# Sixteen units in rounded parts, a chain moved to VectorE at the start, and one function moved to GpSimd at the end

## The chip, the cores and the metric

The kernel runs on one core of a Trainium2 chip. The metric is the device time of one execution in microseconds (us). The core's engines are TensorE (PE in the profile, with PEld for its weight loads), VectorE (DVE), ScalarE (ACT), GpSimd (POOL) and SyncE (SP, which starts most DMAs). Each engine works through its own list of instructions in order; an instruction that waits holds up everything behind it on that engine.

## What is computed

Three pieces follow one another: a linear attention with a delta rule, a network with a rational activation, and a network with a squared relu. Cut to what matters:

```python
# q, k, v: (4, 8, 768, 48); beta: (4, 8, 768)
k_n = k / (norm(k, axis=-1) + 1e-6)
for t in range(768):                       # state: (4, 8, 48, 48)
    y[t]  = q[t] @ state
    state = state + beta[t] * outer(k_n[t], v[t] - k_n[t] @ state)
x = y.transpose(0, 2, 1, 3).reshape(3072, 384)
# network 1: w_in (384, 2048), w_out (2048, 384)
h = x @ w_in
P = a0 + a1*h + a2*h**2 + a3*h**3
Q = 1 + |b0|*|h| + |b1|*h**2
x = (P / (Q + 1e-6)) @ w_out
# network 2: its own w_in, w_out of the same shapes
out = relu(x @ w_in)**2 @ w_out
```

## The kernel before

**Tiles and units.** The 3072 tokens are 6 tiles of 512; the 2048 hidden columns are 16 units of 128. For each tile and unit, the h product (`mm1`, L932) makes a 128x512 block of h in a PSUM bank, an elementwise chain turns it into g, and a second product (`mm2_1`) adds g times the unit's slice of w_out to three banks that hold the tile's output. I write "unit 5.0" for unit 0 of tile 5; tiles are numbered 0 to 5, so tile 5 is the last. Network 2 does the same with a shorter chain, after network 1's last tile.

**Rounded parts.** TensorE multiplies full fp32 operands slowly. So an operand is split into a rounded part and the remainder, each of which is in a faster format, and a product is three products of parts: the h product is 9 matmuls of 128x512 (six with `xh`, three with `xl`). The second product of network 1 is done in one of two ways. In the f32 form (L983) it is three full fp32 matmuls, which the trace counts as six. In the parts form (L986) it is nine, and needs `ph` (ACT, L966) and `pl` = g - ph (POOL, L967), and the parts of w_out, `E` and `F`. The table `QS` says, for each four units, from which tile on the parts form is used: units 0 to 3 from tile 1, units 4 to 11 from tile 2, and units 12 to 15 never.

**The chain of network 1** (`rational`), for each tile and unit: |h| on ACT (L949); its linear function b = b1|h| + b0 on ACT (L950); c = a linear function of h on ACT or DVE (L952, L357); b times |h| on POOL (L955); two DVE instructions on c (L956, L957); Ln and Exp on ACT for 1/Q (L958, L959); three DVE instructions that end with g (L960, L961, L962). L962 is also the last to read the h bank, so the bank is free for another h product then.

**Attention** is cut into groups of 8 steps. Each group's keys are normalised (L477 to L487, on DVE, the longest L486), a small triangular inverse is built step by step (L494 and L498, on POOL for all groups but the first), goes out through memory and comes back transposed as `TN` (L337 on SP), and then TensorE forms W (L570) and T21 (L584), on which the attention steps rest. These steps are spread over tiles 0 to 4.

**Weights.** Network 1's `raw` and network 2's `raw` and `rb` buffers are loaded by DMA as words and split into parts: a copy and a shift (L867, L868), merges on DVE (L872, L876), rounded copies on ACT (L881, L889), subtractions on POOL (L883, L890).

**What sets the order.** A planner (class `Plan`) takes each task with its engine, an assumed cost, a due time and the buffers that it needs, plays the program several times and fixes each engine's order in advance; the program is then written out in that order. Shared buffers, PSUM banks among them, are given out by the planner too. A change in a cost, an engine or a due time so moves many instructions.

Of the kernel before, what the change touches and what calls it, by code (L numbers as in the profile page):

```python
# [36 lines left out]
QS = (1, 2, 2)  # L37
# [8 lines left out]
def tm(u):  # L46

    return T0 + U1 * u if u < 96 else T2 + U2 * (u - 96)
# [192 lines left out]
def kernel(ctx, tc, kT, kS, qT, kn, vn, beta, par_in, w1, w2, outT):  # L241
# [40 lines left out]

    def words(kind, q):
        return lambda: held(kind, q, f"Q{q}", [128, 2 * DM], w1.dtype)[:, :]
# [14 lines left out]
    home = {0: 2, 5: 0, 6: 1, 7: 3}  # L299
    PL.pool("raw2", [lambda y=y: late["raw"][y] for y in range(2)] + [words("rb", q) for q in range(4)])  # L300
    for j, q in home.items():
        slot["raw", 2, j] = PL.pools["raw2"][2 + q]
        PL.gives["raw", 2, j] = [("raw2", 2 + q)]

# [537 lines left out]
    def weights(l, j, due, duo, slack):  # L842
# [7 lines left out]
        wait = [] if l == 1 else [PL.last["late"]] if j not in home else free2[(7, 11, 0, 15)[home[j]]] if j else parts  # L850
# [36 lines left out]
        if l == 2:  # L887
            used[rk] = [len(PL.tasks) - 1, len(PL.tasks) + 1]
            add("ACT", 0.52, lambda: A_.copy(late["C"][j][:, si], res(so)), r=[rk, "late"], w=[("C", j)], due=duo)  # L889
            add("POOL", 1.15, lambda: P_.tensor_tensor(late["C"][j][:, so], res(so), late["C"][j][:, si], op=ALU.subtract),  # L890
                r=[rk], w=[("C", j)], due=duo, lock=1, free=[rk])

# [49 lines left out]
    def rational(i, j, due):  # L942
# [7 lines left out]
        add("ACT", 0.83, lambda: A_.activation(b(), a(), AF.Identity, bias=s(4), scale=s(5)), r=[ak, "par"], w=[bk], due=due + 3.3, alloc=(("b",), bk))  # L950
# [21 lines left out]
    def mm2_1(i, j, due):  # L972
        gk, pk, mk = ((x, (i, j, 1)) for x in ("g", "ph", "pl"))
        two = i >= SJ.get(j, NT)
        if two and i == SJ[j]:
            add("ACT", 0.52, lambda: A_.copy(Ew(j), Bw(j)), r=[("B", j), "pairs"], w=[("E", j)] + [("B", x) for x in range(4 * (j // 4) - 4, 4 * (j // 4)) if x >= 0], due=due - 3)
            add("POOL", 1.15, lambda: P_.tensor_tensor(late["F"][j], Bw(j), Ew(j), op=ALU.subtract), r=[("B", j), ("E", j)], w=[("F", j)], due=due - 2, lock=1)
            parts.append(len(PL.tasks) - 1)
        for d in range(NK):
            def go(d=d):  # L980
                e = slice(128 * d, 128 * d + 128)
                if not two:
                    M.matmul(acc[d], Bw(j)[:, e], slot[gk], start=(j == 0), stop=(j == NJ - 1))  # L983
                    return
                for m, (a, b) in enumerate(((Ew(j)[:, e], slot[mk][0]), (late["F"][j][:, e], slot[pk][0]), (Ew(j)[:, e], slot[pk][0]))):
                    M.matmul(acc[d], a, b, start=(j == 0 and m == 0), stop=(j == NJ - 1 and m == 2))  # L986
# [33 lines left out]
    def pairs():  # L1020
# [4 lines left out]
        late["F"] = {j: sp.tile([128, DM], F32R, name=f"F{j}") for j in SJ}  # L1025
# [38 lines left out]
    for j in range(NJ):  # L1064
        weights(2, j, tm(96 + j) - 3, tm(96 + j) + 9, SA - SB * j)
# [91 lines left out]
```

## Time and profile before

| what | value |
|---|---|
| median of 3 runs | 1034.88 us (1034.8 to 1035.22) |
| the profiled execution | 1035.71 us |
| its span, first to last instruction | 1034.0 us |
| mean granted TensorE clock | 0.965 of full speed |
| PE busy | 976.6 us, 94% |
| DVE / ACT / POOL busy | 689.8 / 597.8 / 450.7 us |
| first h product of the last tile starts | 556.43 us |
| third h product of network 2 starts | 636.28 us |

The times of the rows are microseconds from the span's start. The profiled execution is 0.83 us above the median, and 1.7 us of it lie outside its span.

### The profile page before, as it was taken

What the parts mean: (1) busy time and instruction counts of PE and PEld (TensorE: products, weight loads), DVE (VectorE), ACT (ScalarE), POOL (GpSimd) and SP (SyncE); (2) the same over time, 40 slices, a digit from 0 to 9 for tenths busy, and PEclk for the clock granted to TensorE, in tenths of its full rate; (3) what the DMA queues carried; (4) which work ended last, traced back from release to release, by engine and by line L of the source; (5) the groups of instructions that cost most, each with busy time, mean ns of one, the idle gap of its engine ahead of it and who ended that gap; (6) DMA issues with size and microseconds to landing.
All of it is one profiled execution on the core that took longest, in us unless ns stands there. A gap on an engine that the chain in (4) does not pass through costs nothing.

```text
span 1034.0 us, 23206 instructions
## 1 busy us (share of the span) xinstructions
PE 976.6 (94%) x9532; PEld 754.2 (73%) x9532; DVE 689.8 (67%) x1129; ACT 597.8 (58%) x1047; POOL 450.7 (44%) x543
## 2 busy tenths in 40 slices
PE   4675999999999999999999998999999999999998
PEld 4574666577568867877886765888888888888886
DVE  6888978986788798788885899873343433433332
ACT  4465667876677687577766887743242333333322
POOL 1189987598489849954442656630000000000000
PEclk8567999999999999999999999999999999999999
DMA  8674568315803541250103016500010000000000
GB/s 246 175 212 125 111 207 223 61 53 152 158 33 83 156 71 50 72 124 32 34 5 126 1 54 238 198 30 32 1 61 1 28 35 1 20 11 1 31 1 31
DMA packets 126922, 84.84 MB, mean 82 GB/s; under 512 B 95648, under 2 KB 111776, under 8 KB 126816
## 3 DMA queue, kind: packets, MB, share of 16 engines
q1 hardware_dynamic: 126688, 83.26, 29.4%
q8 instruction: 75, 1.23, 0.5%
q14 instruction: 31, 0.25, 0.1%
q10 hardware_dynamic: 128, 0.10, 0.0%
HBM read 63.54 MB, written 18.61 MB: 79 GB/s over the span
## 4 chain that ended last, share of the span: by engine, by line
PE 75%; DVE 8%; POOL 6%; issue 5%; ACT 3%; DMA 2%; SPq 1%; ACTq 0%; POOLq 0%; DVEq 0%
PE bank L932 32%; PE bank L986 9%; PE bank L667 8%; PE bank L1015 6%; PE bank L1013 6%; PE bank L1014 6%; PE bank L983 6%; POOL mem L955 2%; DVE Tt L498 1%; DVE tmp L494 1%; POOL Tt L498 1%; POOL tmp L494 1%; PE bank L570 1%; POOL pl L967 1%; SPq L337 1%
## 5 line engine op out<-in xcount | busy, mean ns | idle before, releaser
L932 PE MATMUL bank<-xh,A 128*128 128x512 f32 x1152 | 311.8, 406 | 13.4 <-DVE mem L962 8.0
L932 PEld LDWEIGHTS bank<-xh,A 128*128 128x128 f32 x1152 | 217.0, 190 | 78.3 <-issue 10.6
L955 POOL TENSOR_TENSOR mem<-mem 128x512 f32<-128x512 f32 x96 | 126.1, 1314 | 116.5 <-ACT mem L950 114.8
L1001 DVE SCALAR_TENSOR_TENSOR mem<-bank,mem 128x512 f32<-128x512 f32 x96 | 66.2, 689 | 149.5 <-ACT mem L1000 149.1
L932 PE MATMUL bank<-xl,A 128*128 128x512 f32 x576 | 163.3, 392 | 0.0
L1000 ACT ACTIVATE mem<-bank 128x512 f32<-128x512 f32 x96 | 57.5, 598 | 154.0 <-PE bank L932 153.9
L983 PE MATMUL bank<-mem,B 128*128 128x512 f32 x264 | 127.0, 613 | 2.9 <-DVE mem L962 2.9
L932 PEld LDWEIGHTS bank<-xl,A 128*128 128x128 f32 x576 | 109.0, 189 | 23.3
L1015 PE MATMUL bank<-gh,C 128*128 128x512 f32 x288 | 113.8, 395 | 0.0
L1004 DVE TENSOR_TENSOR gl<-mem,gh 128x512 fp32r<-128x512 f32 x96 | 71.3, 744 | 63.4 <-ACT gh L1003 63.3
L1013 PE MATMUL bank<-gl,C 128*128 128x512 f32 x288 | 113.5, 394 | 0.0
L1014 PE MATMUL bank<-gh,C 128*128 128x512 f32 x288 | 111.9, 389 | 0.0
L1003 ACT CAST gh<-mem 128x512 fp32r<-128x512 f32 x96 | 59.6, 621 | 75.8 <-DVE mem L1001 62.0
L498 POOL TENSOR_TENSOR Tt<-Tt,tmp 128x31 f32<-128x31 f32 (+15 forms) x155 | 88.1, 568 | 9.8
L494 POOL TENSOR_TENSOR tmp<-Gb,Tt 128x31 f32<-128x31 f32 (+15 forms) x155 | 84.3, 544 | 16.8 <-DVE nT L485 7.9
L960 DVE SCALAR_TENSOR_TENSOR mem<-mem,par,bank 128x512 f32<-128x512 f32 x96 | 71.2, 742 | 27.0 <-ACT bank L959 26.3
L949 ACT ACTIVATE mem<-bank 128x512 f32<-128x512 f32 x96 | 56.9, 593 | 52.7 <-PE bank L932 39.4
L958 ACT ACTIVATE mem<-mem,par 128x512 f32<-128x512 f32 x96 | 69.3, 722 | 29.0 <-POOL mem L955 28.5
L983 PEld LDWEIGHTS bank<-mem,B 128*128 128x128 f32 x264 | 48.9, 193 | 48.5 <-issue 39.0
L956 DVE TENSOR_TENSOR mem<-bank,mem 128x512 f32<-128x512 f32 x96 | 65.8, 686 | 20.5 <-ACT mem L952 10.5
L950 ACT ACTIVATE mem<-mem,par 128x512 f32<-128x512 f32 x96 | 78.1, 813 | 2.1
L967 POOL TENSOR_TENSOR pl<-mem,ph 128x512 fp32r<-128x512 f32 x52 | 67.5, 1299 | 26.3 <-ACT ph L966 13.9
(129 smaller groups left out, 1725.9 us busy)
## 6 DMA issues: line engine op xcount, KB each, us to landing
raw<-in_w_dram SPq DMA_DIRECT2D x16, 768.0 KB, 6.1
rb<-in_w_dram SPq DMA_DIRECT2D x10, 768.0 KB, 4.5
X<-in_qT_dram SPq DMA_DIRECT2D x48, 112.0 KB, 2.9
gs<-Gs SPq DMA_DIRECT2D x40, 128.0 KB, 2.8
kn<-in_kn_dram SPq DMA_DIRECT2D x12, 384.0 KB, 4.5
vn<-in_vn_dram SPq DMA_DIRECT2D x12, 384.0 KB, 4.2
y<-mem SPq DMA_DIRECT2D x18, 256.0 KB, 2.0
out_dram<-mem SPq DMA_DIRECT2D x18, 256.0 KB, 2.0
```

What stands on the lines that cost most here:

```text
L494: E_.tensor_tensor(tv, _mid(Gb[:, s, s + 1:32], [128, a, b]), Tt[:, 0:a, s:s + 1].to_broadcast([128, a, b]), op=ALU.mult)
L498: E_.tensor_tensor(Tt[:, 0:a, s + 1:32], Tt[:, 0:a, s + 1:32], tv, op=ALU.subtract)
L667: M.matmul(*y[:3], start=a, stop=z)
L932: M.matmul(h, a, b, start=(m == 0), stop=(m == len(seq) - 1))
L950: add("ACT", 0.83, lambda: A_.activation(b(), a(), AF.Identity, bias=s(4), scale=s(5)), r=[ak, "par"], w=[bk], due=due + 3.3, alloc=(("b", ...
L955: add("POOL", 1.32, lambda: P_.tensor_tensor(b(), b(), a(), op=ALU.mult), r=[ak], w=[bk], due=due + 4.2, lock=1)
L967: add("POOL", 1.3, lambda: P_.tensor_tensor(slot[mk][0], g(), slot[pk][0], op=ALU.subtract), r=[gk, pk], w=[mk], due=due + 11.5, lock=1, a ...
L983: M.matmul(acc[d], Bw(j)[:, e], slot[gk], start=(j == 0), stop=(j == NJ - 1))
L986: M.matmul(acc[d], a, b, start=(j == 0 and m == 0), stop=(j == NJ - 1 and m == 2))
L1013: M.matmul(acc[d], wh, gl, start=(j == 0), stop=False)
L1014: M.matmul(acc[d], wl, gh, start=False, stop=False)
L1015: M.matmul(acc[d], wh, gh, start=False, stop=(j == NJ - 1))
```

## The change

Five things are edited.

1. `QS` gets a fourth entry, 3: units 12 to 15 use the parts form from tile 3 on, so in tiles 3, 4 and 5. Their `E` and `F` lie in storage that other weights have left (`Fw`), and are made in tile 3's reach with two buffers of the attention as scratch.
2. In tile 0, for units 0 to 2, the product b times |h| goes to DVE instead of POOL.
3. In the last tile the linear function of |h| goes to POOL (`tensor_scalar`) instead of ACT.
4. The normalisation of attention group 2 waits for the tasks in the list `opened`, which held only the splitting of tile 0's x; the g of units 0.0 and 0.1 is added to it (`OPEN`). And the attention's tasks are entered one tile further ahead.
5. Network 2's unit 0 of weights is loaded early into the first part of `xin`, the buffer of network 1's x, after the last tile's x has been split; the x of network 2's first tile, which goes there too, waits for its use.

```diff
-QS = (1, 2, 2)
+QS = (1, 2, 2, 3)
+OPEN = 2
+X0 = 83
...
+    def Fw(j):
+        return held("F", 3, "Q3", [128, 4 * DM], F32R)[:, DM * (j - 12):DM * (j - 12) + DM] if j > 11 else late["F"][j]
...
-    home = {0: 2, 5: 0, 6: 1, 7: 3}
+    home = {5: 0, 6: 1, 7: 3, 8: 2}
...
+    xw = xin.rearrange("p k n -> p (k n)")[:, 0:1536]
+    slot["raw", 2, 0] = xw.bitcast(w1.dtype) if f64 else xw[:, :2 * DM]
...
+        if i == NT - 1:
+            add("POOL", 1.3, lambda: P_.tensor_scalar(b(), a(), s(5), s(4), op0=ALU.mult, op1=ALU.add), r=[ak, "par"], w=[bk], due=due + 3.3, lock=1, alloc=(("b",), bk))
+        else:
+            add("ACT", 0.83, lambda: A_.activation(b(), a(), AF.Identity, bias=s(4), scale=s(5)), r=[ak, "par"], w=[bk], due=due + 3.3, alloc=(("b",), bk))
...
-        add("POOL", 1.32, lambda: P_.tensor_tensor(b(), b(), a(), op=ALU.mult), r=[ak], w=[bk], due=due + 4.2, lock=1)
+        dv = i == 0 and j < 3
+        add("DVE" if dv else "POOL", 0.69 if dv else 1.32, lambda: (V if dv else P_).tensor_tensor(b(), b(), a(), op=ALU.mult), r=[ak], w=[bk], due=due + 4.2, lock=1)
...
+        if i == 0 and j < OPEN:
+            opened.append(len(PL.tasks) - 1)
...
-        if two and i == SJ[j]:
+        if two and i == SJ[j] and j == 12:
...
+            for x in range(12, 16):
+                keys = [("Gb", 0, o) for o in (0, 32, 64, 96)] if x < 14 else [("Tt", 0)]
+                add("ACT", 0.52, lambda x=x: A_.copy(Ew(x), Bw(x)), r=[("B", x), "pairs"], w=[("E", x)] + [("B", y) for y in range(8, 12)], due=due - 9)
+                add("POOL", 1.15, lambda x=x: P_.tensor_tensor(T[x - 12], Bw(x), Ew(x), op=ALU.subtract), r=[("B", x), ("E", x)], w=keys, due=due - 8, lock=1)
...
+                add("ACT", 0.52, lambda x=x: A_.copy(Fw(x), T[x - 12]), r=keys, w=[("F", x)] + over, due=due - 5)
...
+    attention(0)
     for i in range(NT):
-        attention(i)
-        attn_last = len(PL.tasks)
         split(i, 1, tm(16 * i) - 3)
+        if i < NT - 1:
+            attention(i + 1)
+            attn_last = len(PL.tasks)
```

**How it moves instructions.** Lines after the change are numbered higher by 7 at the attention (L486 becomes L493, L570 L577, L584 L591), by 9 at the h product (L932 becomes L941), by 13 in the chain (L955 becomes L968, L962 L975), L966 and L967 become L981 and L982, and L983 and L986 become L1008 and L1011.

The first place is the opening of tile 0 on DVE. `bank_74` and `bank_72` hold the h of units 0.0 and 0.1, `Gb_120` the keys of attention group 2. Before, in part:

```order
L956 TENSOR_TENSOR mem<-bank_74,mem 128x512
L477 RECIPROCAL nbr<-tmp_124 128x32
...
L486 TENSOR_TENSOR Gb_120<-Gb_120,nbr 128x1024
L487 COPY Tt_122<-nbr 128x32
L485 STREAM_TRANSPOSE nT_131<-tmp_124 128x32
L957 SCALAR_TENSOR_TENSOR mem<-mem,par,bank_74 128x512
```

After the change:

```order
L969 TENSOR_TENSOR mem<-bank_74,mem 128x512
L968 TENSOR_TENSOR mem<-mem 128x512
L970 SCALAR_TENSOR_TENSOR mem<-mem,par,bank_74 128x512
L968 TENSOR_TENSOR mem<-mem 128x512
L969 TENSOR_TENSOR mem<-bank_72,mem 128x512
...
L975 SCALAR_TENSOR_TENSOR mem<-bank_74,mem 128x512
L975 SCALAR_TENSOR_TENSOR mem<-bank_72,mem 128x512
L484 RECIPROCAL nbr<-tmp_124 128x32
```

The normalisation now stands behind the g of both units, and DVE makes the products b times |h| (L968) itself.

The same place on PE. `A_85`, `A_86` and `A_87` are the weights of units 0.1, 0.2 and 0.3, and `TT`, `TN` belong to the attention's W. Before, the first matmul of each product and what follows:

```order
L932 MATMUL bank_72<-xh_100,A_85 128x512 x2
...
L932 MATMUL bank_73<-xh_100,A_86 128x512 x2
...
L932 MATMUL bank_74<-xh_100,A_87 128x512 x2
...
L932 MATMUL bank_73<-xl_105,A_89 128x512
L570 MATMUL bank_76<-TT_118,TN 32x32 x64
```

After the change:

```order
L941 MATMUL bank_72<-xh_100,A_85 128x512 x2
...
L941 MATMUL bank_74<-xh_100,A_86 128x512 x2
...
L941 MATMUL bank_72<-xh_100,A_87 128x512 x2
...
L1008 MATMUL bank_71<-mem,B_923 128x512
L577 MATMUL bank_75<-TT_118,TN 32x32 x64
L941 MATMUL bank_74<-xh_100,A_88 128x512 x2
```

Unit 0.2 now takes bank 74, which unit 0.0 must have left, where it had a third bank; and W comes two h products (units 0.4 and 0.5) earlier in the order, before unit 0.4 instead of after unit 0.5.

The second place is the turn from tile 4 to the last tile on PE. Before, the last h product of tile 4 ends in `bank_72`, and these follow it up to the last tile's first h product in `bank_76`; `E_3402`, `F` and `B_2202` are slices of w_out. In part:

```order
L932 MATMUL bank_72<-xl_105,A_99 128x512
L986 MATMUL bank_69<-pl_2397,E_3402 128x512
...
L986 MATMUL bank_70<-ph_2396,E_3402 128x512
L983 MATMUL bank_69<-mem,B_2202 128x512
...
L983 MATMUL bank_70<-mem,B_2202 128x512
L932 MATMUL bank_76<-xh_100,A_84 128x512 x2
```

There stand 15 matmuls of the parts form and 12 of the f32 form (4 units), so that tile 4 is complete before tile 5 starts. After the change:

```order
L941 MATMUL bank_72<-xl_105,A_99 128x512
L1011 MATMUL bank_69<-pl_2444,E_3544 128x512
...
L1011 MATMUL bank_71<-ph_2443,E_3544 128x512
L941 MATMUL bank_76<-xh_100,A_84 128x512 x2
```

Now 18 matmuls of the parts form (2 units) stand there and none in f32; two more units of tile 4 come after the last tile's first h products.

The third place is the end of the last tile on POOL. Before:

```order
L955 TENSOR_TENSOR mem<-mem 128x512
L967 TENSOR_TENSOR pl_2397<-mem,ph_2395 128x512
L955 TENSOR_TENSOR mem<-mem 128x512
L967 TENSOR_TENSOR pl_2398<-mem,ph_2396 128x512
L955 TENSOR_TENSOR mem<-mem 128x512 x3
L883 TENSOR_TENSOR A_84<-rb_3496,A_84 128x384
```

After:

```order
L960 TENSOR_SCALAR mem<-mem,par 128x512
L968 TENSOR_TENSOR mem<-mem 128x512
L982 TENSOR_TENSOR pl_2444<-mem,ph_2442 128x512
L982 TENSOR_TENSOR pl_2445<-mem,ph_2443 128x512
...
L890 TENSOR_TENSOR A_85<-raw_0_6801,A_85 128x384
L982 TENSOR_TENSOR pl_2444<-mem,ph_2442 128x512
L890 TENSOR_TENSOR A_86<-raw_1_6802,A_86 128x384
L897 TENSOR_TENSOR C_6780<-raw_0_6801,C_6780 128x384
L982 TENSOR_TENSOR pl_2445<-mem,ph_2443 128x512
```

From the first linear function (L960) to that last `pl`, POOL has 16 linear functions, 16 products (L968), 17 subtractions for `pl` (L982) and 5 subtractions for weights of network 2 (L890, L897).

## Rows read from the trace of the kernel before

**Rows 1.** The page, busy time of each engine, share of the span and instructions.

```profile
PE 976.6 (94%) x9532; PEld 754.2 (73%) x9532; DVE 689.8 (67%) x1129; ACT 597.8 (58%) x1047; POOL 450.7 (44%) x543
```

**Rows 2.** Windows of tiles 3, 4, 5: length, busy PE, PEld, DVE, ACT, POOL; clock.

```profile
375.90:464.90 89.00, 87.84 (x1187) 67.57 (x1185) 74.64 (x127) 62.19 (x106) 69.89 (x92) 1.00 0.29 72
464.90:556.40 91.50, 91.34 (x923) 68.11 (x918) 74.08 (x123) 64.02 (x110) 35.95 (x28) 1.00 0.10 30
556.40:628.70 72.30, 66.90 (x271) 50.58 (x269) 62.06 (x87) 63.59 (x102) 39.75 (x31) 0.98 0.18 61
```

**Rows 3.** The chain that ended last, in tile 4: start, us, what.

```profile
476.54 2.58 PE bank L983 x6
479.11 2.08 PE bank L932 x9
481.19 2.04 PE bank L986 x9
483.24 2.04 PE bank L932 x9
```

**Rows 4.** PE's waits from 85 to 640: us in total, times, longest.

```profile
PE bank L932 <- DVE mem L962: 8.0, 3, 7.4
PE bank L986 <- POOL pl L967: 3.9, 4, 2.0
```

**Rows 5.** Timeline of PE in the opening of tile 0.

```profile
99.69 2.93 PE L932 MATMUL bank<-xh,A 128*128 128x512 f32 x6 [7.44 <-DVE mem L962]
...
114.41 1.29 PE L570 MATMUL bank<-TT,TN 32*32 32x32 f32 x128
```

**Rows 6.** Timelines of DVE, POOL and SP in the same stretch.

```profile
92.82 2.22 DVE L486 TENSOR_TENSOR Gb<-Gb,nbr 128x1024 f32<-128x1024 f32 x1
...
98.94 0.69 DVE L962 SCALAR_TENSOR_TENSOR mem<-bank,mem 128x512 f32<-128x512 f32 x1
...
92.70 1.27 POOL L955 TENSOR_TENSOR mem<-mem 128x512 f32<-128x512 f32 x1
...
99.97 0.27 POOL L498 TENSOR_TENSOR Tt<-Tt,tmp 128x31 f32<-128x31 f32 x1
...
106.51 2.15 SPq L337 DMA_DIRECT2D TN<-nd  x4
```

**Rows 7.** Groups of instructions in the last tile: busy, mean ns, idle before.

```profile
L955 POOL TENSOR_TENSOR mem<-mem 128x512 f32<-128x512 f32 x16 | 21.0, 1314 | 30.4 <-ACT mem L950 30.4
...
L967 POOL TENSOR_TENSOR pl<-mem,ph 128x512 fp32r<-128x512 f32 x12 | 15.8, 1320 | 10.3 <-ACT ph L966 10.3
...
L950 ACT ACTIVATE mem<-mem,par 128x512 f32<-128x512 f32 x16 | 12.9, 809 | 0.2
...
L957 DVE SCALAR_TENSOR_TENSOR mem<-mem,par,bank 128x512 f32<-128x512 f32 x15 | 11.2, 746 | 0.4
...
L876 DVE SCALAR_TENSOR_TENSOR raw<-raw 128x768 uint32<-128x768 uint32 x2 | 3.6, 1822 | 0.0
...
L356 DVE CAST xh<-xin 128x512 fp32r<-128x512 f32 x3 | 2.7, 924 | 0.0
...
L883 POOL TENSOR_TENSOR A<-raw,A 128x384 fp32r<-128x384 f32 x2 | 2.6, 1336 | 0.8 <-ACT A L881 0.8
```

**Rows 8.** Timeline of PE in the last tile and behind it.

```profile
556.43 1.95 PE L932 MATMUL bank<-xh,A 128*128 128x512 f32 x6
...
615.26 0.50 PE L986 MATMUL bank<-pl,E 128*128 128x512 f32 x1 [1.96 <-POOL pl L967]
...
617.86 2.84 PE L983 MATMUL bank<-mem,B 128*128 128x512 f32 x6 [0.26 <-DVE mem L962]
...
623.00 6.26 PE L983 MATMUL bank<-mem,B 128*128 128x512 f32 x10 [2.29 <-DVE mem L962]
...
636.28 1.95 PE L932 MATMUL bank<-xh,A 128*128 128x512 f32 x6
```

**Rows 9.** Groups of POOL by form, all tiles: its one-operand instruction nearest in size.

```profile
L473 POOL MEMSET Tt<- 128x1024 f32 x6 | 6.0, 1004 | 1.9 <-DMA td<-Tt 1.0 <-DVE TN L516 0.8
```

More of the change, by code (lines that the diff above doesn't have):

```diff
@@ L849, in weights @@
         e = rk in slot
-        wait = [] if l == 1 else [PL.last["late"]] if j not in home else free2[(7, 11, 0, 15)[home[j]]] if j else parts
+        wait = [] if l == 1 else list(x2free[0]) if j == 0 else [PL.last["late"]] if j not in home else free2[(7, 11, 15, 15)[home[j]]]
         over = [i for k in (6, 7) if l == 1 and 4 * (k - 4) <= j < 4 * (k - 3) for i in used["raw", 1, k]]
@@ L891, in weights @@
                 r=[rk], w=[("C", j)], due=duo, lock=1, free=[rk])
+            if j == 0:
+                x2free[0] += [used[rk][0], len(PL.tasks) - 1]
     for j in range(NJ):
@@ L949, in rational @@
         add("ACT", 0.6, lambda: A_.activation(a(), h(), AF.Abs), r=[hk], w=[ak], due=due + 2.5, alloc=(("a",), ak))
-        add("ACT", 0.83, lambda: A_.activation(b(), a(), AF.Identity, bias=s(4), scale=s(5)), r=[ak, "par"], w=[bk], due=due + 3.3, alloc=(("b",), bk))
+        if i == NT - 1:
+            add("POOL", 1.3, lambda: P_.tensor_scalar(b(), a(), s(5), s(4), op0=ALU.mult, op1=ALU.add), r=[ak, "par"], w=[bk], due=due + 3.3, lock=1, alloc=(("b",), bk))
+        else:
+            add("ACT", 0.83, lambda: A_.activation(b(), a(), AF.Identity, bias=s(4), scale=s(5)), r=[ak, "par"], w=[bk], due=due + 3.3, alloc=(("b",), bk))
         if i == NT - 1:
@@ L974, in mm2_1 @@
         two = i >= SJ.get(j, NT)
-        if two and i == SJ[j]:
+        if two and i == SJ[j] and j == 12:
+            over = [("B", x) for x in range(12, 16)]
+            T = [y.rearrange("p a b -> p (a b)")[:, o:o + DM] for y in (Gbs[0], Tts[0]) for o in (0, DM)]
+            for x in range(12, 16):
+                keys = [("Gb", 0, o) for o in (0, 32, 64, 96)] if x < 14 else [("Tt", 0)]
+                add("ACT", 0.52, lambda x=x: A_.copy(Ew(x), Bw(x)), r=[("B", x), "pairs"], w=[("E", x)] + [("B", y) for y in range(8, 12)], due=due - 9)
+                add("POOL", 1.15, lambda x=x: P_.tensor_tensor(T[x - 12], Bw(x), Ew(x), op=ALU.subtract), r=[("B", x), ("E", x)], w=keys, due=due - 8, lock=1)
+            for x in range(12, 16):
+                keys = [("Gb", 0, o) for o in (0, 32, 64, 96)] if x < 14 else [("Tt", 0)]
+                add("ACT", 0.52, lambda x=x: A_.copy(Fw(x), T[x - 12]), r=keys, w=[("F", x)] + over, due=due - 5)
+        if two and i == SJ[j] and j < 12:
             add("ACT", 0.52, lambda: A_.copy(Ew(j), Bw(j)), r=[("B", j), "pairs"], w=[("E", j)] + [("B", x) for x in range(4 * (j // 4) - 4, 4 * (j // 4)) if x >= 0], due=due - 3)
-            add("POOL", 1.15, lambda: P_.tensor_tensor(late["F"][j], Bw(j), Ew(j), op=ALU.subtract), r=[("B", j), ("E", j)], w=[("F", j)], due=due - 2, lock=1)
+            add("POOL", 1.15, lambda: P_.tensor_tensor(Fw(j), Bw(j), Ew(j), op=ALU.subtract), r=[("B", j), ("E", j)], w=[("F", j)], due=due - 2, lock=1)
             parts.append(len(PL.tasks) - 1)
@@ L984, in go @@
                     return
-                for m, (a, b) in enumerate(((Ew(j)[:, e], slot[mk][0]), (late["F"][j][:, e], slot[pk][0]), (Ew(j)[:, e], slot[pk][0]))):
+                for m, (a, b) in enumerate(((Ew(j)[:, e], slot[mk][0]), (Fw(j)[:, e], slot[pk][0]), (Ew(j)[:, e], slot[pk][0]))):
                     M.matmul(acc[d], a, b, start=(j == 0 and m == 0), stop=(j == NJ - 1 and m == 2))
@@ L1024, in pairs @@
         late["E"] = sp.tile([128, 4 * DM], F32R, name="E0")
-        late["F"] = {j: sp.tile([128, DM], F32R, name=f"F{j}") for j in SJ}
+        late["F"] = {j: sp.tile([128, DM], F32R, name=f"F{j}") for j in range(12)}
         for x in ("ph", "pl"):
@@ L1064 @@
     for j in range(NJ):
-        weights(2, j, tm(96 + j) - 3, tm(96 + j) + 9, SA - SB * j)
+        weights(2, j, tm(96 + j) - 3 if j else tm(X0), tm(96 + j) + 9 if j else tm(X0), SA - SB * j if j else 4)
     for i in range(NT):
```

## The prediction

> **What bounds the kernel now.** I read the page's busy times first: TensorE is busy for 976.6 of 1034.0 us [rows 1], so time is won by giving it less work or by closing its gaps. The windows of tiles 3 to 5 come next [rows 2]. In tiles 3 and 4 PE is busy 87.84 of 89.00 and 91.34 of 91.50 us at full clock: there an engine beside it has room, and a microsecond off PE is a microsecond off the time. The last tile is different: PE is busy 66.90 of 72.30, while VectorE has 62.06 and GpSimd 39.75. The chain inside tile 4 [rows 3] prices a unit: an h product 2.08 (2.04 behind a parts product), a second product in f32 2.58 and in parts 2.04. The list of PE's waits from 85 to 640 us [rows 4] has two that matter: 8.0 us for the last instruction of a unit's chain (L962), of which 7.4 at one place, and 3.9 for `pl`. The timelines put the 7.44 into the opening of tile 0 [rows 5] and the others at the end of the last tile (1.96, 0.26 and 2.29), with ten matmuls in 6.26 us where six take 2.58 [rows 3, 8], so ten should take 4.30.
>
> **The change part by part.**
>
> *Parts in tiles 3 to 5.* An f32 unit followed by an h product costs 2.58 + 2.08, a parts unit 2.04 + 2.04 [rows 3], a difference of 0.58. Twelve unit-products change, 12 x 0.58 = 7.0 us. Each adds a `ph` on ScalarE and a `pl` of 1.32 on GpSimd [rows 7], four units a tile: 5.3 us of GpSimd in tiles whose GpSimd is idle for 19 and 55 us [rows 2], and about 3 of ScalarE, idle for 27. The one-time `E` and `F` (four subtractions of about 1.3, eight ACT copies) fall in tile 3's reach: 5 us in those 19. I cost them at nothing. If that cover were gone, 5.3 us of GpSimd per tile would come up as PE waits for `pl`.
>
> *The opening.* Before, the g of unit 0.0 was ready at 98.94 + 0.69 = 99.63 [rows 6]. The normalisation of group 2 (its longest instruction 2.22) stood between its DVE instructions, and its POOL product, 1.27, stood among the steps of group 1's inverse. After, DVE has both units' chains ahead of the normalisation: 13 instructions of about 0.7, some already done by 92. I take 97.7, 2 us sooner. But the order lets PE make only two h products ahead of it, since unit 0.2 takes bank 74, and before it made three. So PE waits from about 90.2 to 97.7, where it waited from 92.25 to 99.69 [rows 5], and one product of 2.08 stands behind the wait instead of ahead of it: 2 won, 2 given back. Then W. Group 1's inverse ended at 99.97 + 0.27 = 100.24, and the last transfer for it was issued 8.4 us later (106.51 + 2.15) [rows 6]. Two or three products of 1.27 leave POOL ahead of it, so it ends near 97. With 8.4 and a landing for which no row stands here (I allow 3), W can start near 108.5. PE gets there through two h products (the first at low clock: six matmuls in 2.93 [rows 5], where they take 1.95 [rows 8], so about 4.4 for the nine), and two f32 units: 97.7 + 4.4 + 2.1 + 5.2 = 109.4. So W does not wait, by less than 1 us, where it had slack to 114.41. I take the opening as 0, with bounds of -3 (the freed time at the start is kept) and +4 (the inverse does not move, and W waits till about 112; one more wait for the third bank).
>
> *The last tile, its start.* It starts at 556.43 [rows 8]. Tile 3's four units bring 2.3, two of tile 4's bring 1.2, and two units of tile 4 are moved behind its first products, 2 x 2.58 = 5.2. So it starts near 547.7, and has two parts units more to do.
>
> *The last tile, its length.* Three queues can end it, counted from its start, to the end of unit 5.15's second product.
> - PE: 17 h products (one of network 2) and 18 parts units, 35 x 2.04 = 71.4.
> - DVE: the window's busy 62.06 [rows 2]; the three casts (2.7) go to ACT, one more merge of weights is in it (1.8), and one unit's four instructions that the window lacks (2.9) come to it [rows 7]: 64.1. It can begin after an h product and two ACT instructions (2.04 + 2 x 0.81 = 3.7), and behind its last g come `ph` (about 0.8), `pl` 1.32 and a parts unit: 64.1 + 3.7 + 0.8 + 1.3 + 2.0 = 71.9. Should a few gaps remain (the window has 10 of them), 77.
> - POOL: 16 products of 1.31, 17 `pl` of 1.32, 5 subtractions of 1.34 [rows 7] and 16 linear functions of x: 50.1 + 16x. It begins one h product and one ACT instruction in (2.85) and a parts unit follows (2.04): 55.0 + 16x. The trace of before has no `tensor_scalar` on POOL. The nearest rows are its two-operand instruction on the same 128x512, 1.31, and a MEMSET of 1024 columns, 1.00, or 0.50 for 512 [rows 9]. I take 1.31, since it reads and computes as the former does and the MEMSET reads nothing; the bound of 0.50 stays for the range. That gives 76.0; from x = 1.06 on POOL decides over DVE.
>
> So second products end near 547.7 + 76.0 = 623.7. One h product of network 2 (unit 1) then brings PE to the point at which before's third h product began: 625.8 against 636.28, 10.5 us. ScalarE loses 16 x 0.81 = 12.9 us of its work there, which decides nothing while POOL is the longest.
>
> The Trainium skill, "GPSIMD Engine Reference", section 3.1, lays the price of a two-input instruction on GpSimd to its two operands taking turns at one read port, and gives 769 ns for a good one-input body over 512 elements. By that figure x would be 0.77 (an estimate), POOL's queue 67.3, and DVE's 71.9 would decide: 4 us better than I forecast. The 1.31 of the row bears out the slow two-input half, and no row here shows a one-input computation.
>
> *Weights of network 2.* Unit 0's words are loaded into `xin` once the last tile's x is split, some 60 us before they are used; the x of network 2's first tile waits for their use. Loads of this kind land in a few us; nothing, unless the use comes late, where each us would be one of PE's.
>
> Sum: 10.5 us off the profiled execution's 1035.71 is 1025.2. That execution stands 0.83 over the median of the runs shown, so 1024.4.
>
> **The rivals.**
> - *GpSimd's linear function is short.* With x at 0.50 POOL's queue is 63.0, DVE (71.9) and PE (71.4) end together, and the gain is 14.6: 1020.3. For it: a single operand. Against it: nothing in the trace reads and computes on POOL faster than 1.31 at this size. The figure of the Trainium skill's "GPSIMD Engine Reference" above is this case.
> - *The opening loses.* Two banks instead of three, and W two products earlier in the order with less than 1 us of slack: up to 4 us, 1028.4. For it: the sum above has no room. Against it: POOL's inverse loses two products.
> - *Slower: the linear function on POOL is longer than the two-operand instruction.* Each 0.1 us over 1.31 adds 1.6 us. The gain is gone at 1.31 + 10.5 / 16 = 1.97; with two passes (2.62) the last tile ends 21 us later, 1045.3, and PE waits for `pl` at each unit. For it: two operations with per-partition scalars, of which no row tells the price. Against it: ScalarE does the same function in one pass of 0.81, and POOL's cost per element elsewhere goes with operands read.
> - *No change: the tile's end keeps its length.* If DVE's gaps and new waits of PE eat the 7 us of tiles 3 to 5 as well, DVE's queue would have to end 86 after the tile's start, 14 more than its work. Little speaks for it: 1035.
>
> **How the numbers follow.** The forecast (POOL's queue decides, opening neutral) has 0.55, the short function 0.2, the opening that loses 0.13, slower 0.07, no change 0.05. A measurement of this kernel tells 0.2%, 2.1 us, from no change. The forecast's own range is 1021 to 1027 (DVE's 77, or two microseconds at low clock as in before's tail). The 8 in 10 range goes from below the short function's 1020.3, where an opening that wins could add a part of its 3, up to the losing opening with a slow tail: 1018.5 to 1030.5. Faster by over 0.2%: 0.55 + 0.2 + 0.13 = 0.88; the others 0.05 and 0.07.
>
> **What would show it.** In the profile after, tiles 3 and 4 should show no f32 product of units 12 to 15 and PE without new waits; the last tile's first h product should start near 548 (near 552 if the opening loses 4); the window from there to the last second product should be 76 long with POOL at over 90%, and PE's waits there for `pl`. A `tensor_scalar` mean on POOL near 1.3 shows the sum right, near 0.5 to 0.8 the first rival, above 2 the third. In the opening, one wait of PE for L975 of about 7.5 ahead of unit 0.2, and W near 109 without a wait. The prediction is wrong if PE waits at W, or if network 2's third h product starts later than 631.

## The result, and the profile after

The change takes 1027.52 us (median of 4 runs, 1025.13 to 1027.85) where the kernel before took 1035.05 on the same chip: a ratio of 0.991, 95% interval 0.9895 to 0.9925 (the quotient of the two medians alone is 0.9927). By the medians that is 7.5 us faster; 10.5 was forecast, and the time lies in the range that was given. Executions of one kernel lie 3 us and more apart here. The reasons are another matter: the experiments below take them apart.

The page of the changed kernel gives the busy times, as [rows 1]:

```profile
PE 971.6 (95%) x9568; PEld 764.1 (74%) x9568; DVE 691.0 (67%) x1127; ACT 598.2 (58%) x1056; POOL 480.5 (47%) x572
```

The windows of tile 3, of tile 4, and from the last tile's first h product to network 2's second tile (columns as in [rows 2]: length, busy PE, PEld, DVE, ACT, POOL, then the granted clock):

```profile
377.10:465.20 88.10, 87.43 (x1190) 68.17 (x1188) 73.37 (x125) 65.44 (x113) 72.09 (x95) 1.00 0.30 72
465.20:548.70 83.50, 83.50 (x923) 68.65 (x922) 68.83 (x115) 65.77 (x114) 40.34 (x32) 1.00 0.13 42
548.70:685.90 137.20, 132.91 (x571) 107.82 (x570) 121.25 (x157) 101.14 (x175) 100.46 (x83) 0.99 0.33 113
```

I call the stretch of the last two rows the tail: tile 4's first h product to network 2's second tile. It takes 220.8 us after (685.94 less 465.15). Before, the same stretch is 91.5 and this row, so 229.2:

```profile
556.40:694.10 137.70, 131.88 (x542) 101.66 (x541) 116.78 (x151) 106.36 (x178) 77.91 (x60) 0.99 0.33 112
```

So about 8.5 us of the gain are in the tail. The stretch from the first h product to tile 4 takes 379.4 in this profile and 381.3 before, and the first h product itself starts 2.2 us later (85.80 against 83.61). What of these two small terms belongs to the change is asked below.

In the opening, the timeline of PE answers to [rows 5] and that of DVE to [rows 6]:

```profile
100.16 2.92 PE L941 MATMUL bank<-xh,A 128*128 128x512 f32 x6 [7.31 <-DVE mem L975]
...
111.97 1.29 PE L577 MATMUL bank<-TT,TN 32*32 32x32 f32 x128
```

```profile
99.42 1.28 DVE L975 SCALAR_TENSOR_TENSOR mem<-bank,mem 128x512 f32<-128x512 f32 x2
```

The wait is as long as before (7.31 against 7.44), one product earlier in the order, and W follows without a wait. Counted from the first h product it ends 14.4 us in, where before it ended after 16.1.

The groups of the last tile, from its first h product to its last second product (busy, mean ns of one, idle before):

```profile
L968 POOL TENSOR_TENSOR mem<-mem 128x512 f32<-128x512 f32 x17 | 23.3, 1373 | 4.0 <-ACT mem L962 3.0
...
L960 POOL TENSOR_SCALAR mem<-mem,par 128x512 f32<-128x512 f32 x16 | 12.3, 769 | 0.5 <-ACT mem L958 0.5
...
L925 DVE TENSOR_TENSOR xl<-xin,xh 128x512 fp32r<-128x512 f32 x3 | 4.7, 1606 | 0.0
```

The linear function takes 0.769 us on GpSimd, not 1.31. And GpSimd's product, which waited 30.4 us for ScalarE's L950 before [rows 7], waits 4.0. Not all of the 30.4 is of one kind: 14.6 of it is a single wait at the tile's start, as the list of GpSimd's waits before shows (us in total, times, longest).

```profile
POOL mem L955 <- ACT mem L950: 30.4, 14, 14.6
```

The tile's end, in timelines of PE, DVE and ACT:

```profile
617.83 0.51 PE L941 MATMUL bank<-xl,A 128*128 128x512 f32 x1 [1.19 <-DVE xl L925]
619.25 0.50 PE L941 MATMUL bank<-xl,A 128*128 128x512 f32 x1 [0.92 <-DVE xl L925]
...
623.72 0.56 PE L1011 MATMUL bank<-pl,E 128*128 128x512 f32 x1 [1.91 <-POOL pl L982]
```

```profile
614.53 4.67 DVE L925 TENSOR_TENSOR xl<-xin,xh 128x512 fp32r<-128x512 f32 x3
619.12 0.73 DVE L973 SCALAR_TENSOR_TENSOR mem<-mem,par,bank 128x512 f32<-128x512 f32 x1
```

```profile
621.28 0.62 ACT L981 CAST ph<-mem 128x512 fp32r<-128x512 f32 x1 [3.85 <-DVE mem L975]
```

These lines form a chain. Network 2's three remainders stand on DVE ahead of the last unit's three instructions; ScalarE waits 3.85 for that unit's g, GpSimd then makes `pl`, and PE waits for it. The chain that ended last shows what follows on PE: nine matmuls take 3.92 us instead of 2.04, with a mean granted clock of 0.56 from 623.72 to 627.60, near the lower level of 1.2 GHz. In the 6.7 us before, PE was busy for 3.06.

```profile
623.72 3.92 PE bank L1011 x9
627.63 4.09 PE bank L941 x18
```

### The profile page after: what moved, and what is told of

The parts are those of the page before. It is cut to its first block, busy times and chain, and to the rows that moved or that the text cites. A ratio compares the mean times of both kernels' runs of the same rounds, so it can differ in the third digit from the quotient of the medians.

```text
span 1025.8 us, 23327 instructions
## 1 busy us (share of the span) xinstructions
PE 971.6 (95%) x9568; PEld 764.1 (74%) x9568; DVE 691.0 (67%) x1127; ACT 598.2 (58%) x1056; POOL 480.5 (47%) x572
## 4 chain that ended last, share of the span: by engine, by line
PE 74%; POOL 9%; DVE 9%; ACT 3%; issue 2%; SPq 1%; DMA 1%; ACTq 0%; POOLq 0%; DVEq 0%
PE bank L941 32%; PE bank L1011 11%; PE bank L674 7%; PE bank L1040 7%; PE bank L1038 6%; PE bank L1039 6%; POOL tmp L501 2%; POOL Tt L505 2%; PE bank L1008 2%; POOL mem L968 2%; POOL pl L982 1%; DVE Tt L505 1%; DVE tmp L501 1%; SPq L344 1%; DVE mem L973 1%
## 5 line engine op out<-in xcount | busy, mean ns | idle before, releaser
L941 PE MATMUL bank<-xh,A 128*128 128x512 f32 x1152 | 309.1, 404 | 14.1 <-DVE mem L975 9.0
L941 PEld LDWEIGHTS bank<-xh,A 128*128 128x128 f32 x1152 | 218.0, 191 | 74.8 <-DVE mem L975 11.4
L941 PE MATMUL bank<-xl,A 128*128 128x512 f32 x576 | 163.8, 392 | 2.1 <-DVE xl L925 2.1
L968 POOL TENSOR_TENSOR mem<-mem 128x512 f32<-128x512 f32 x93 | 122.1, 1313 | 72.3 <-ACT mem L962 69.3
L941 PEld LDWEIGHTS bank<-xl,A 128*128 128x128 f32 x576 | 109.0, 189 | 26.1 <-DVE xl L925 2.9
L982 POOL TENSOR_TENSOR pl<-mem,ph 128x512 fp32r<-128x512 f32 x64 | 84.1, 1314 | 23.7 <-ACT ph L981 21.9
L1008 PE MATMUL bank<-mem,B 128*128 128x512 f32 x192 | 91.0, 603 | 0.0
L971 ACT ACTIVATE mem<-mem,par 128x512 f32<-128x512 f32 x96 | 69.2, 722 | 24.3 <-POOL mem L968 24.0
L1011 PE MATMUL bank<-pl,E 128*128 128x512 f32 x192 | 79.1, 412 | 3.0 <-POOL pl L982 2.6
L1011 PE MATMUL bank<-ph,F 128*128 128x512 f32 x192 | 75.8, 395 | 0.0
L1011 PE MATMUL bank<-ph,E 128*128 128x512 f32 x192 | 75.5, 393 | 0.0
```

Source lines behind the costliest of these rows:

```text
L941: M.matmul(h, a, b, start=(m == 0), stop=(m == len(seq) - 1))
L968: add("DVE" if dv else "POOL", 0.69 if dv else 1.32, lambda: (V if dv else P_).tensor_tensor(b(), b(), a(), op=ALU.mult), r=[ak], w=[bk], ...
```

## The experiments

Their times lie close together, so the tail of one profile each is compared too. It is the stretch that repeated when the change was profiled twice (below); of the others there is one profile, and those of `no_xl` and `no_dve_products` are of executions some 3 us under their medians, so their tails are to be read with that in mind. The starts are those of the h products in the timelines. Each ratio is to the kernel before on the same chip, where its median was 1035.05 to 1036.45.

| kernel | median us | ratio to before, 95% | first h product | to tile 4 | tail |
|---|---|---|---|---|---|
| before | 1035.05 | | 83.61 | 381.3 | 229.2 |
| the change | 1027.52 | 0.991 (0.9895 to 0.9925) | 85.80 | 379.4 | 220.8 |
| change_again | 1029.58 | 0.9935 (0.9922 to 0.9948) | 85.12 | 381.8 | 220.8 |
| no_lin | 1035.64 | 1.0004 (0.999 to 1.0018) | 85.14 | 381.5 | 227.3 |
| no_parts | 1028.0 | 0.9927 (0.9912 to 0.9942) | 84.85 | 380.3 | 220.1 |
| lin_only | 1026.95 | 0.9913 (0.9896 to 0.9929) | 85.17 | 380.6 | 220.1 |
| no_dve_products | 1025.81 | 0.99 (0.9874 to 0.9926) | 84.33 | 378.9 | 218.3 |
| no_xl | 1027.11 | 0.991 (0.9886 to 0.9934) | 85.53 | 380.9 | 216.0 |
| no_parts_no_xl | 1027.71 | 0.9928 (0.9911 to 0.9944) | 85.74 | 379.9 | 220.2 |
| two_units | 1029.04 | 0.9923 (0.9895 to 0.9951) | 86.02 | 382.2 | 218.9 |
| xl_gpsimd | 1036.3 | 1.0 (0.9988 to 1.0012) | 85.67 | 383.3 | 227.1 |
| best | 1025.58 | 0.9891 (0.9878 to 0.9905) | 85.20 | 378.9 | 219.8 |
| no_opening | 1100.46 | 1.062 (1.0602 to 1.0637) | | | |
| parts_only | 1111.49 | 1.0719 (1.0685 to 1.0752) | | | |

The theory at the outset was the prediction's: the parts' 7 us of TensorE time are the gain, and the end of the last tile gives some back.

### The opening taken back, and the parts alone

```diff
-        dv = i == 0 and j < 3
+        dv = False
...
-OPEN = 2
+OPEN = 0
...
-    attention(0)
     for i in range(NT):
+        attention(i)
+        attn_last = len(PL.tasks)
         split(i, 1, tm(16 * i) - 3)
-        if i < NT - 1:
-            attention(i + 1)
-            attn_last = len(PL.tasks)
```

`no_opening` is this; `parts_only` has the last tile's linear function back on ScalarE as well.

> The change without edits 2 and 4 (tile 0's products back on GpSimd, the attention's order and the normalisation as before). Theory: the opening as changed wins nothing; its profile has the first h product at 85.8 where before had 83.6, and tile 1 starts 0.9 later than before. Then this kernel has the first h product near 83.6, tile 1 near 193, and is as fast as the change or up to 1.5 us faster. Rival: the opening did pay; then tile 1 starts 2 or more us later than 193.8 and the time is 2 to 4 us above the change's.

> The kernel before with edits 1 and 5 alone. Theory: nearly all of the gain is TensorE time that f32 products gave up, 7 us at 0.58 per unit-product; then 5 to 8 us under before. Rival: the gain needs the linear function's move, since ScalarE also gets twelve more copies; then under 4 us.

Both missed by some 70 us and more, for a reason that none of the expectations had: neither kernel is a test of the opening. GpSimd's waits from 200 to 560 us in `no_opening`:

```profile
POOL Tt L480 <- ACT F L999: 15.4, 1, 15.4
```

L480 clears the buffer in which attention group 4 builds its inverse, and it waits for ScalarE's copies of `F` for units 12 to 15 (L999), which read that same buffer as scratch. In the change the last such clearing starts at 261.6 us, here at 393.8. While it waits, everything behind it on GpSimd waits too: tile 2 takes 126.6 us from first h product to first h product (the change 90.7), and tile 3 107.6 (88.1). With attention group 4 entered after tile 3's units, the scratch of those units stands ahead of it. That the order is what costs the time is shown by `no_dve_products` below, which differs from `no_opening` in the attention's order alone and takes 1025.81. That it does so through edit 1's scratch is read from this wait, and it is not all: tile 0, long before it, is longer too, 124.4 us (the change 108.0), for a reason that was not looked for.

From tile 4 on the two can still be compared. The tail is 221.7 us in `no_opening`, about that of the change, and 231.5 in `parts_only`: the linear function's place alone is 9.8 us there.

### The linear function back on ScalarE

```diff
-        if i == NT - 1:
+        if False:
             add("POOL", 1.3, lambda: P_.tensor_scalar(b(), a(), s(5), s(4), op0=ALU.mult, op1=ALU.add), r=[ak, "par"], w=[bk], due=due + 3.3, lock=1, alloc=(("b",), bk))
```

> The change without edit 3 (the linear function of the last tile stays on ScalarE). ScalarE then has some 62 + 13 = 75 us of work in the 77 us up to the last second product, GpSimd 67.6 - 12.3 = 55. Theory: what ends the tile late is the order at its end (three splits of network 2's x on VectorE, weight subtractions on GpSimd), not the queue that holds the linear function; then the time stays within 1.5 us of the change's. Rival: ScalarE becomes the longest queue; then the stretch from the last tile's first h product to the last second product grows from 78.8 to 81 or more, and the time by 2 to 4 us.

1035.64 us, the time of before: the rival, and by more than it said. All parts are in, and they bring 2 us of tail. The stretch from the last tile's first h product:

```profile
550.30:693.90 143.60, 135.35 (x571) 108.23 (x570) 126.96 (x162) 110.46 (x185) 87.61 (x67) 0.98 0.31 108
```

PE has the same 571 records as after the change, waits 8.2 us in it instead of 4.3, and is busy 2.4 us longer at a lower mean clock.

### The parts taken out

```diff
-QS = (1, 2, 2, 3)
+QS = (1, 2, 2)
```

> The change without edit 1 (units 12 to 15 stay f32 everywhere). Theory: as the 7 us of TensorE time are the gain, the time comes back to within 1.5 us of before. Rival: the opening and the end of the last tile carry a part of it; then 2 to 5 us under before.

1028.0: the theory missed again, and beyond the rival as well. Without a single one of the twelve unit-products in parts the kernel is as fast as the change. The row of the same stretch:

```profile
550.30:685.30 135.00, 135.00 (x557) 103.94 (x556) 119.68 (x158) 97.78 (x168) 94.24 (x77) 1.00 0.33 115
```

PE is busy all of the time, at full clock. With f32 there is no wait to be had there; with parts there are 4.3 us of waits and PE falls to a lower clock after them.

### One edit on the kernel before

`lin_only` is the kernel before with edit 3 and nothing else:

```diff
-        add("ACT", 0.83, lambda: A_.activation(b(), a(), AF.Identity, bias=s(4), scale=s(5)), r=[ak, "par"], w=[bk], due=due + 3.3, alloc=(("b",), bk))
+        if i == NT - 1:
+            add("POOL", 1.3, lambda: P_.tensor_scalar(b(), a(), s(5), s(4), op0=ALU.mult, op1=ALU.add), r=[ak, "par"], w=[bk], due=due + 3.3, lock=1, alloc=(("b",), bk))
+        else:
+            add("ACT", 0.83, lambda: A_.activation(b(), a(), AF.Identity, bias=s(4), scale=s(5)), r=[ak, "par"], w=[bk], due=due + 3.3, alloc=(("b",), bk))
```

> The kernel before with edit 3 alone (the last tile's linear function on GpSimd). The runs so far say that parts bring nothing without it (1035.64) and that the change without parts is as fast as the change (1028.0). Theory: edit 3 is the gain, since it frees ScalarE, on which VectorE and GpSimd wait at the end of the last tile; then 5 to 9 us under before. Rival: edits 2, 4 and 5 carry it (the early weights, the attention's order, the opening); then under 2 us.

1026.95 us: this one edit is as fast as all five. Its row of the stretch is to be held against before's 137.70 above, at nearly the same number of records:

```profile
557.30:685.90 128.60, 128.60 (x543) 101.65 (x542) 114.40 (x149) 95.40 (x164) 92.39 (x76) 1.00 0.35 120
```

9.1 us shorter: 5.8 of waits are gone (137.70 less 131.88), and 3.3 of PE's busy time, 2.0 of which were the ten matmuls at low clock [rows 8]. ScalarE's work in it falls from 106.36 to 95.40.

How the move does this is less plain than that it does. Up to about the tile's last g the rows are, before and in `lin_only`:

```profile
556.40:632.60 76.20, 70.80 (x284) 53.29 (x283) 65.81 (x92) 65.26 (x105) 43.57 (x34) 0.98 0.20 67
557.35:625.80 68.45, 68.45 (x286) 53.49 (x285) 60.94 (x91) 55.28 (x92) 55.76 (x50) 1.00 0.27 96
```

The stretch is 7.8 us shorter. VectorE's gaps in it shrink by 2.9, most of which it had waited for ScalarE's Exp:

```profile
DVE mem L960 <- ACT bank L959: 4.0, 4, 1.4
DVE mem L963 <- ACT bank L962: 1.5, 3, 0.8
```

The other 4.9 is work that VectorE no longer has: two of the three casts of x went to ScalarE (1.7), and the preparation of weights (L868, L876) takes 3.3 less for the same number. So a part of the gain may come from the planner's new order at the tile's end and not from ScalarE's shorter list as such; no run held the order and moved only the function.

The lists of instructions of this kernel and of before are the same on every engine until the last tile (line numbers aside). Yet its first h product starts at 85.17, before's at 83.61. So a start later by 1.6 us is no effect of an edit.

### The opening without VectorE's products

```diff
-        dv = i == 0 and j < 3
+        dv = False
...
-OPEN = 2
+OPEN = 0
```

> The change without edit 2 and without the wait for the first two units, but with the attention entered a tile ahead. Theory: the opening is neutral; within 1.5 us of the change, and its profile has the first h product later than before's 83.6, since that comes of the attention's new order. Rival: VectorE's products pay; 2 to 4 us slower than the change, with a longer wait of PE for the first g.

1025.81, 1.7 us under the change's median on another chip and so a little beyond the 1.5 that the theory allowed (the ratios to before overlap), but not the slower time of the rival. The rest of the theory, that the attention's new order makes the first h product late, fell with `lin_only`. Edit 2 and the wait of edit 4 bring nothing that these runs can show.

### The remainders left out, with and without parts

```diff
             either(0.62, 0.6, lambda k=k, s=s: (xh[k], s()), r=xr, w=[("xh", k)], due=due)
+            if l == 2 and i == 0:
+                continue
             add("DVE", 0.75, lambda k=k, s=s: V.tensor_tensor(xl[k], s(), xh[k], op=ALU.subtract), r=xr + [("xh", k)], w=[("xl", k)], due=due, lock=1)
```

> The change with the three remainders (xl) of network 2's first tile left out: that tile is then multiplied with the remainders of network 1's last tile, so part of the computation is left out. In the change's profile they take 4.67 us of VectorE, 1.6 each, right ahead of the last unit's three instructions, and ScalarE waits 3.85 for the last g. Theory: VectorE is the queue that ends the last tile; then the last g is 3 to 5 us earlier and the time 3 to 5 us shorter. Rival: the order of GpSimd at the end (weight subtractions between the last two subtractions for pl) decides; then under 1.5 us.

The tail falls by 4.8 us, 220.8 to 216.0, but the theory's own two signs fail: the median of the time (1027.11) is that of the change, and the last g, at 621.2, is 71.2 us after the tile's start where it was 72.5, only 1.3 earlier. In the place of the remainders VectorE now prepares weights, ahead of the same three instructions:

```profile
615.81 1.85 DVE L883 SCALAR_TENSOR_TENSOR rb<-rb 128x768 uint32<-128x768 uint32 x1
617.58 1.65 DVE L875 TENSOR_SCALAR rb<-rb 128x768 uint32<-128x768 uint32 x1
```

The rest of the shorter tail is in PE's row: 1.4 us of waits for 4.3 (2.1 of these were for the remainders themselves), and 1.9 less of busy time, the low clock behind the waits.

```profile
550.00:682.50 132.50, 131.06 (x572) 106.71 (x572) 118.35 (x154) 101.06 (x175) 100.49 (x83) 1.00 0.33 117
```

The same cut in the kernel without parts asks whether VectorE is the bound in both forms:

```diff
-QS = (1, 2, 2, 3)
+QS = (1, 2, 2)
```

> The change without edit 1, and with the three remainders (xl) of network 2's first tile left out, as in the run that kept the parts (part of the computation is left out). From tile 4's start to network 2's second tile the change took 220.7 and 220.8 us in two profiles, without parts 220.1 with PE busy all of the last stage, and with parts and without the remainders 216.0. Theory: with f32 TensorE is the bound there and VectorE only with parts, so relief of VectorE brings nothing here: 219.5 to 220.5. Rival: VectorE sets the pace of the stretch in both forms; then about 4.7 less, 215 to 217.

220.2 us of tail: nothing, as the theory had it. With f32 PE is busy for 135.09 of 135.10 us, and relief of VectorE goes unused. In the time the two cuts do not differ (1027.11 with parts, 1027.71 without, each 0.991 to 0.993 of before).

```profile
550.70:685.80 135.10, 135.09 (x557) 104.09 (x556) 116.53 (x155) 98.35 (x168) 90.36 (x77) 1.00 0.32 115
```

### Two attempts at a better end

`two_units` keeps units 14 and 15 in f32 and puts `E` and `F` of units 12 and 13 into one quarter:

```diff
-SJ = {j: QS[j // 4] for j in range(4 * len(QS))}
+SJ = {j: QS[j // 4] for j in range(14)}
...
-        return held("F", 3, "Q3", [128, 4 * DM], F32R)[:, DM * (j - 12):DM * (j - 12) + DM] if j > 11 else late["F"][j]
+        return held("E", 3, "Q2", [128, 4 * DM], F32R)[:, DM * (j - 10):DM * (j - 10) + DM] if j > 11 else late["F"][j]
...
-            for x in range(12, 16):
+            for x in range(12, 14):
```

> The change with units 12 and 13 alone in parts from tile 3 on; units 14 and 15 stay f32, so the last tile ends without their ph and pl. Theory: without parts PE was busy for 135.0 of 135.0 us from the last tile's start to network 2's second tile, with all of them it waited for 4.3; half of the parts takes 3.5 us of PE work and leaves the end of the tile its short chain; then 2 to 4 us faster than the change, 1023.5 to 1025.5. Rival: any unit in parts adds to VectorE's, ScalarE's and GpSimd's queues as much as it takes from PE; then the change's time within 1 us.

The tail is 218.9, 1.9 better, but the stretch to tile 4 took 382.2 and the time (1029.04) is not better than the change's: the theory of 2 to 4 us missed.

`xl_gpsimd` gives the three remainders to GpSimd:

```diff
+            if l == 2 and i == 0:
+                add("POOL", 1.3, lambda k=k, s=s: P_.tensor_tensor(xl[k], s(), xh[k], op=ALU.subtract), r=xr + [("xh", k)], w=[("xl", k)], due=due, lock=1)
+                continue
```

> The change with the three remainders (xl) of network 2's first tile made by GpSimd instead of VectorE. GpSimd was busy for 67.6 of 77.1 us up to the last second product, VectorE for 74.3. Theory: VectorE ends the last tile; it is relieved of 4.7 us and GpSimd gets 3.9, which it has room for: the stretch from tile 4's start to network 2's second tile shrinks from 220.7 by 2 to 4 us. Rival: GpSimd and VectorE get in each other's way at the end, or GpSimd's longer list delays the last pl; then it stays within 1 us or grows.

1036.3, the whole gain gone. The end of the last tile is the place: PE's waits from 83 to 700 us have a new entry behind the old 7.3 of the opening, network 2's weights that GpSimd prepares.

```profile
PE bank L944 <- POOL A L890: 6.4, 2, 4.9
PE bank L944 <- ACT xh L359: 3.9, 1, 3.9
PE bank L944 <- POOL xl L926: 2.2, 2, 1.2
```

The line in the middle is the wait ahead of the first h product, which every kernel here has (3.7 before, 4.4 after).

The rival, in a form that the expectation had only in part: what is late is not `pl` but the weights for the next h products, and the row of the stretch has a granted clock of 0.96.

### The change once more, and the best

`change_again` is the change unaltered.

> The change itself once more, to see how much of a profile repeats. Theory: the time until the first h product differs between executions by one or two us (83.6 to 86.0 in the runs so far, whatever the edit), and the stretch from the first h product to network 2's second tile repeats within 1 us of the change's 600.1. Rival: the change's opening is what makes the first h product late; then it starts at 85.8 again, and the stretch from tile 4's start to network 2's second tile may differ as well.

The tail repeats to 0.1 us (220.8 twice), its three remainders take 4.67 us again; the stretch to tile 4 does not (379.4 and 381.8), so my bound of 1 us for the sum was too narrow. A difference of 2 us ahead of tile 4 is therefore nothing to explain.

`best` is `no_dve_products` with `xl_gpsimd`'s edit and the planner's cost of the linear function as measured:

```diff
-            add("POOL", 1.3, lambda: P_.tensor_scalar(b(), a(), ...
+            add("POOL", 0.77, lambda: P_.tensor_scalar(b(), a(), ...
```

> The change without VectorE's products in tile 0 and the wait for the first two units, with xl of network 2's first tile on GpSimd, and with the planner's cost of the linear function at 0.77, as measured, instead of 1.3. Theory: from the first h product to network 2's second tile 594 to 597 us (the change 600.1, without the opening's edits 597.2, with xl left out 597.0); 2 to 5 us faster than the change. Rival: the new order costs what the relief brings; the change's time within 1.5 us.

598.7 us from the first h product to network 2's second tile, above what I expected, and a tail of 219.8, no better than that of `no_dve_products`. Its median of 1025.58 is 4.0 us under that of the change on the same chip (1029.58), in the 2 to 5 that I expected, and the intervals of the two ratios do not meet. But its ratio to before overlaps with that of `no_dve_products`, so this is no proof for the moved remainders, and which of its edits brings the 4.0 was not taken apart.

## Why the prediction was right, and where it was wrong

**The number** held, 3.1 us from the forecast, within a range of 12. What carries it is not what I said, and that it came so near is in part luck.

**The start of the last tile** was right: 547.7 was forecast and 548.7 measured. Tiles 3 and 4 took 171.6 us for 180.5 before, 8.9 less, where the sum had 8.7 (most of it work moved behind the tile's start).

**Its length** is where the microseconds are missing. Network 2's third h product starts at 629.52, 80.8 after the tile's start; 78.1 was forecast (625.8 less 547.7), and before it was 79.9. The tile did not get 1.8 us shorter but 1.0 longer.

```profile
629.52 1.52 PE L941 MATMUL bank<-xh,A 128*128 128x512 f32 x6
```

**The step that failed** is in that length: "ScalarE loses 16 x 0.81 = 12.9 us of its work there, which decides nothing while POOL is the longest." That move alone, on the kernel before, is 9.1 us of tail and about 9 of the time (ratio 0.9913), and without it the other four edits bring nothing (1.0004). I had added up three queues (PE, DVE, POOL) and left ScalarE's out. In the kernel before GpSimd's product waited for ScalarE's linear function at 14 of 16 units [rows 7]; I had that row in hand and read it as slack of GpSimd. Of its 30.4 us, 14.6 are the idle start of the tile, which `lin_only` keeps: there GpSimd's linear function waits 14.0 in all, 13.8 of it once. The other 15.8, in 13 waits, are all but gone.

```profile
L951 POOL TENSOR_SCALAR mem<-mem,par 128x512 f32<-128x512 f32 x16 | 12.9, 806 | 14.0 <-ACT mem L949 14.0
```

That the place of the linear function is the gain is shown by `lin_only` and `no_lin`, and again by `parts_only` held against `no_opening`. That ScalarE's queue held the chain, with 8.7 us of idle time left in its window (63.59 of 72.30, [rows 2]), by delaying each unit's next step, is my reading; the planner's new order, which also took 4.9 us of work from VectorE, is a rival that no run rules out.

**Parts, 7.0 us.** The size was nearly right as work and wrong as time. Without parts PE is busy for 85.10 + 135.00 = 220.1 us in the tail, with parts and without the remainders for 83.50 + 131.06 = 214.6: 5.5 less. The traces have 66 f32 matmuls of second products in the tail without parts, which are eleven units, and none with them; by 0.58 each that should give 6.4. Tile 4 in these two kernels:

```profile
465.20:550.30 85.10, 85.10 (x909) 65.37 (x905) 67.63 (x114) 64.97 (x110) 35.18 (x28) 1.00 0.13 41
466.50:550.00 83.50, 83.50 (x926) 68.67 (x922) 68.70 (x115) 65.76 (x114) 40.22 (x32) 1.00 0.13 42
```

"A microsecond off PE is a microsecond off the time" was read in tiles 3 and 4, where PE hardly waits; whatever they win, the last tile has to be short enough to keep. With the linear function moved, the f32 kernel fills PE to the last microsecond, and with parts VectorE is the longer queue, busy for 69.69 of the 72.50 us up to the last g. In the tails of one profile each, leaving out the remainders is worth 4.8 with parts and nothing without; the medians of the time do not show it.

**DVE's queue.** Forecast: 64.1 us of work and the last g 67.8 after the tile's start. It came 72.5 after (621.2 less 548.7), with 69.69 of work. The row of that stretch, and two of VectorE's groups in it:

```profile
548.70:621.20 72.50, 70.12 (x306) 56.82 (x305) 69.69 (x98) 59.06 (x100) 63.81 (x55) 1.00 0.21 66
L975 DVE SCALAR_TENSOR_TENSOR mem<-bank,mem 128x512 f32<-128x512 f32 x18 | 12.4, 690 | 0.6
L974 DVE SCALAR_TENSOR_TENSOR bank<-mem,bank 128x512 f32<-128x512 f32 x18 | 12.3, 686 | 0.0
```

The largest term that the sum lacks is tile 4's: I moved two of its units behind the tile's start in PE's queue, but not what VectorE still had to do for them. Each of the five chain instructions stands there 17 or 18 times where I had 16, seven more in all, about 4.9 us. The three remainders are the second: they were in the window of before, at 0.96 each, and take 1.61 each beside a busy GpSimd, 1.9 more.

```profile
L916 DVE TENSOR_TENSOR xl<-xin,xh 128x512 fp32r<-128x512 f32 x3 | 2.8, 958 | 0.0
```

The rule that VectorE ends the tile when the linear function is short was a rival at 0.2, and its gain was set too high, 14.6, since DVE's term was too low.

**POOL's queue.** The term x was taken as 1.31 and is 0.769, so the queue is 67.3 by my own sum, not 76.0. The forecast's mechanism (GpSimd as the longest) is wrong. The tile's second products end 78.9 us after its start, near the 76.0, because VectorE's term (71.9) was 7.0 too low and GpSimd's 8.7 too high: that is the luck. The Trainium skill, "GPSIMD Engine Reference", section 3.1, gives 769 ns as measured for 512 elements in its best case, below what it states for two inputs; the mean of the change's trace agrees with it (769 ns), and with it the first rival's condition was met.

**The opening** was forecast as 0 and is 0: the wait has 7.31 us against 7.5, W follows the two f32 units ahead of it without a wait, and the kernel without VectorE's products is no slower.

**The rival of no change** (0.05) spoke of the right thing, the tile's end eating what tiles 3 to 5 win; that is what the parts' 7 us met in `no_lin`, while edit 3 paid in their place.

**Not costed at all:** edit 4's order. Without it the scratch of edit 1 stands in front of an attention group, and the kernel is 73 us slower than the change and 65 slower than before.

## What to carry to other kernels

A wait of an idle engine for another engine's step that comes back at nearly every unit can point at the queue that sets the pace, even if the engine waited for has an eighth of its time idle; take out the one long wait at the start of a stage first. Sum up every engine's queue, above all the one that is waited for, and count in it the work that a stage inherits from the one before. A saving on the engine that looks like the bound is only kept if the last stage can follow; try each edit alone, for here one of five was the gain and one of the others was needed merely so that another did no harm. Where a planner fixes the order, an edit also moves other work, so what an edit is worth and why are two questions. And compare stretches that repeat between two profiles of the same kernel before a microsecond is explained.

## What the runs showed of the hardware

A `tensor_scalar` on GpSimd over 128x512 takes 0.77 us on average in the change, its two-operand instruction 1.37 in the same tile and 1.31 in the last tile of the kernel before. The 0.77 is not met everywhere: the mean is 0.81 in `lin_only` and 0.90 in `no_parts`, where three of the sixteen took 1.3 to 1.5.

The remainder `xl`, a VectorE instruction with two operands in SBUF, takes 1.61 us on average at the end of the last tile with GpSimd at work beside it; in the kernel before, one at 623.52 us had GpSimd idle and took 0.69:

```profile
623.52 0.69 DVE L916 TENSOR_TENSOR xl<-xin,xh 128x512 fp32r<-128x512 f32 x1
```

VectorE's instructions with an operand in PSUM keep their time there (L970 of the change has 746 ns, L957 of before 746 in [rows 7]). GpSimd pays as well: `pl` takes 1.74 us beside the remainders, and 1.30 in the one before them at 611.12.

```profile
615.49 1.74 POOL L982 TENSOR_TENSOR pl<-mem,ph 128x512 fp32r<-128x512 f32 x1
```

The Trainium skill, "GPSIMD Engine Reference", section 8, says that GpSimd shares its SBUF interfaces with VectorE and contends with VectorE's instructions that have two SBUF inputs; these rows agree.
